# Two more row tiles of a spectral and feed-forward kernel normalised and multiplied in 64-row halves, one weight block loaded once, and the input loaded ahead of the constants

## The chip, the core and the metric

The kernel runs on one core of one Trainium2 chip. A core has TensorE (PE in the profile; its weight loads are PEld), VectorE (DVE), ScalarE (ACT), GpSimd (POOL) and SyncE (SP), which here only issues transfers. Each engine works through its instructions in a fixed order; semaphores make one wait for another. SBUF (128 partitions) holds the data, PSUM (8 banks of 128 x 512 float32) takes what TensorE computes, and DMA engines move data. The metric is the device time of one execution in microseconds; lower is better.

## The reference

Two equal layers are applied to x of shape 1 x 2048 x 448 in bfloat16. Each adds a filter in the frequency domain and then a feed-forward block (FFN), both after a layer normalisation without gain:

```python
def _A_ref(x, w_r, w_i):
    X = jnp.fft.rfft2(x.astype(jnp.float32), axes=(-2, -1))
    X = X * (w_r + 1j * w_i)
    return jnp.fft.irfft2(X, s=(S, D), axes=(-2, -1)).astype(jnp.bfloat16)

def _B_ref(x, w1, b1, w2, b2):
    h = jnp.einsum("bsd,df->bsf", x, w1) + b1
    h = relu(h) ** 2
    return jnp.einsum("bsf,fd->bsd", h, w2) + b2

for layer in range(2):
    x = x + _A_ref(_layernorm(x), w_r, w_i)
    x = x + _B_ref(_layernorm(x), w1, b1, w2, b2)
```

S is 2048, D is 448, and the hidden width F is 1792 = 14 x 128.

## The kernel before

The 2048 rows are 16 row tiles of 128 rows. The transforms are matmuls with constant matrices (FA, TD, G, H, TI, FI and others) that are loaded at the start. The program goes through these stages:

- Start (0 to 17.7 us). The rows of x come into `xin` by four transfers on SP's queue and four on ACT's. Per tile: statistics (DVE, L825, or ACT, L847), a reversed copy XR (POOL, L707, into `VT`), a scaled constant `Fs` (POOL L718 or ACT L717), and five matmuls with it (stage A1).
- Spectral 1 (to 42.6 us): matmuls with TD, G and H, and between them products with the filter on DVE.
- Ramp 1 (to 50.2 us). Inverse stages TI and AI return x per pair of tiles: TI's matmuls, an eviction of 128 x 896 to `tmp` (ACT, L706), AI's matmuls, and a sum into `x_sb` (DVE, L1146). Then `ln_B` normalises.
- FFN 1 (to about 142 us). Rows go in four chunks of four tiles. `h_part` or `h_pairs` make the hidden rows of a chunk (14 blocks `fb` of 128 features), ACT applies ReLU, DVE squares, and `o_tile` multiplies a row tile by W2 in 14 matmuls of 448 columns.
- Spectral 2, ramp 2 (142 to 172.9 us) and FFN 2 (to 262.7 us), the same once more; rows leave at the end.

The first FFN matmul needs its rows transposed, in `yT`: four blocks of 128 columns per tile, the fourth with only 64 columns of data. Three ways lead there:

- Tiles 0 and 1: raw rows are flipped on TensorE by matmuls with J (`flip`) and evicted to `yT`. They are not normalised. The standard deviation and its rounding rest stand in two extra columns of x (L1163 on), so that b1 is added by two more rows of W1, and the output tile is multiplied by the squared reciprocal deviation (`r2`).
- Tiles 2 and 3: raw in the same way, but transposed by one DMA from `x_sb` on SP's queue.
- Tiles 4 to 15: `ln_rows` takes the root, the reciprocal, scales each tile into the buffer `xn` (it lies in `arena`, room for one pair), copies the 64 tail columns once more behind the row, and sends one DMA transpose per pair. The fourth block of `yT` then has its 64 rows in both partition halves.

`h_part` uses raw rows with 128-row blocks: four matmuls per block `fb`, each with two tiles (256 columns) as the moving operand. `h_pairs` uses normalised rows and splits the contraction of 448 into seven blocks of 64 rows, so that two matmuls, one on the lower and one on the upper half of the array, stand side by side; all four tiles (512 columns) move through, and b1 is added as a bias by the ReLU. For the fourth block the upper half needs rows 384 to 447 of W1 on partitions 64 to 127 (`W1u`). Before, these lie in `VT`, which the spectral stage uses, so that they are loaded again in each layer, by two transfers on SP's queue behind the transpose of tiles 6 and 7.

The order of each engine's instructions is not found by rule: a table `ORDER` holds, per engine, the numbers of the program's units, and the scheduler replays it. It picks the PSUM banks, adds the semaphore waits, and inserts dummy matmuls on `ones` (L1415) where it expects TensorE to idle. The table also sets the order of transfers on SP's queue and which engine evicts where two are allowed.

## Time and profile before

| What | Value |
|---|---|
| Runs | 266.54 us median of 3 (266.14 to 266.84) |
| Profiled execution | 266.92 us |
| Its span | 265.0 us |
| PE busy | 256.8 us (97%) |
| DVE busy | 204.5 us (77%) |
| ACT busy | 172.7 us (65%) |
| First matmul of FFN 1, of FFN 2 | 50.17 us, 172.87 us |
| Granted TensorE clock | 1.00 in every stretch |

The span is what the profiler recorded between the first and the last instruction; the execution's time has 1.9 us around it. PE's busy time includes pipelined matmuls, so the distance between two starts, and not the duration in a row, is what a matmul costs in a stream. In a timeline row the first number is the start, the second the time to the end of the group, and brackets give the idle time before it and what ended it.

### The profile page before, as it was taken

The numbers are of one execution on the slowest core, as the hardware profiler recorded it, in microseconds if no ns is written. First come the engines' busy times: TensorE is split into PE (matmuls) and PEld (weight loads), VectorE is DVE, ScalarE is ACT, GpSimd is POOL, SyncE is SP. The second block draws the span as 40 slices with busy tenths as digits, with TensorE's granted clock in tenths as the row PEclk, the third lists the DMA queues.
The fourth block names the chain that finished last, engine by engine and source line by source line (L and its number), as shares of the span: only waits on it lengthen the run. The fifth ranks groups of instructions, "written<-read, shape, count | busy, mean of one in ns | idle before, by whom it ended". The sixth has DMA issues, their size and how long they took to land.

```text
span 265.0 us, 5666 instructions
## 1 busy us (share of the span) xinstructions
PE 256.8 (97%) x2125; PEld 162.6 (61%) x2125; DVE 204.5 (77%) x658; ACT 172.7 (65%) x375; POOL 14.2 (5%) x32
## 2 busy tenths in 40 slices
PE   6999989999999999999999999999999999999996
PEld 2676768797544555665558756789654465554454
DVE  2978998999969983489998899899964069921662
ACT  5978897999449447893216889999634886121820
POOL 8840000000000000000000000000000000000000
PEclk9999999999999999999999999999999999999999
DMA  7999900032300214000000000022232000220053
GB/s 223 303 299 385 270 8 2 0 72 41 74 2 1 44 37 80 2 0 2 0 1 2 2 0 2 0 45 41 42 69 45 2 0 2 40 41 2 0 173 106
DMA packets 25531, 16.33 MB, mean 62 GB/s; under 512 B 18174, under 2 KB 24542, under 8 KB 25504
## 3 DMA queue, kind: packets, MB, share of 16 engines
q1 hardware_dynamic: 24768, 14.25, 19.9%
q10 hardware_dynamic: 576, 0.92, 1.0%
q0 software_dynamic: 160, 0.81, 0.9%
q8 instruction: 17, 0.28, 0.4%
q14 instruction: 10, 0.08, 0.1%
HBM read 10.46 MB, written 1.84 MB: 46 GB/s over the span
## 4 chain that ended last, share of the span: by engine, by line
PE 81%; DVE 8%; ACT 5%; DMA 2%; issue 2%; SPq 0%; POOL 0%; DVEq 0%; POOLq 0%
PE ps L681 81%; DVE tmp L735 6%; DMA xin<-in_A_x_dram 2%; DVE arena L735 2%; ACT VT L706 2%; ACT tmp L706 2%; ACT arena L706 1%; SPq L673 0%; ACT yT L706 0%; ACT mv L700 0%; DVE st L825 0%; PE ps L1415 0%; ACT Fs L717 0%; POOL Fs L718 0%; DVE VT L707 0%
## 5 line engine op out<-in xcount | busy, mean ns | idle before, releaser
L681 PE MATMUL ps<-yT,W_sb 64*128 64x512 bf16 (+1 forms) x770 | 90.3, 346 | 0.1
L681 PE MATMUL ps<-W_sb,arena 128*128 128x448 bf16 (+3 forms) x476 | 87.0, 342 | 0.0
L681 PEld LDWEIGHTS ps<-yT,W_sb 64*128 64x128 bf16 (+1 forms) x770 | 54.5, 95 | 31.9 <-ACT arena L700 1.3
L700 ACT ACTIVATE arena<-ps,b1col 128x512 bf16<-128x512 f32 x84 | 51.9, 689 | 28.8 <-PE ps L681 28.8
L681 PEld LDWEIGHTS ps<-W_sb,arena 128*128 128x128 bf16 x476 | 45.4, 98 | 38.5 <-DVE arena L735 1.5
L735 DVE TENSOR_TENSOR arena<-arena 128x512 bf16<-128x512 bf16 (+1 forms) x140 | 45.8, 366 | 24.7 <-ACT arena L700 24.5
L706 ACT ACTIVATE arena<-ps 128x448 bf16<-128x448 f32 (+1 forms) x41 | 26.0, 705 | 4.5 <-PE ps L681 4.4
L1170 ACT ACTIVATE VT<-x_sb 128x448 bf16<-128x448 bf16 x28 | 16.1, 580 | 16.4 <-DVE x_sb L1146 16.4
L700 ACT ACTIVATE mv<-mv,epst 128x1 f32<-128x1 f32 (+1 forms) x45 | 12.6, 296 | 17.0 <-DVE mv L826 14.0
L700 ACT ACTIVATE arena<-ps 128x256 bf16<-128x256 f32 x56 | 18.0, 386 | 0.6 <-PE ps L681 0.5
L706 ACT ACTIVATE XA<-ps 128x512 bf16<-128x512 f32 x26 | 14.5, 590 | 5.2 <-PE ps L681 5.1
L681 PE MATMUL ps<-arena,G_sb 128*128 128x448 bf16 (+1 forms) x84 | 16.9, 335 | 0.9 <-ACT arena L706 0.9
L1292 DVE SCALAR_TENSOR_TENSOR x_sb<-ps,mv,arena 128x448 bf16<-128x448 f32 (+2 forms) x13 | 8.3, 644 | 11.9 <-PE ps L681 11.8
L681 PE MATMUL ps<-H_sb,arena 128*128 128x256 bf16 x128 | 15.8, 273 | 1.2 <-DVE arena L735 0.6
L706 ACT ACTIVATE VT<-ps 128x1024 bf16<-128x1024 f32 (+2 forms) x20 | 14.0, 773 | 3.0 <-PE ps L681 3.0
L735 DVE TENSOR_TENSOR tmp<-arena,Wt 128x896 bf16<-128x896 bf16 x26 | 15.4, 623 | 0.6 <-ACT arena L706 0.4
L681 PE MATMUL ps<-yT,VT 64*128 64x512 bf16 x42 | 15.8, 376 | 0.0
L681 PEld LDWEIGHTS ps<-H_sb,arena 128*128 128x128 bf16 x128 | 11.7, 98 | 5.0 <-DVE arena L735 3.4
L681 PE MATMUL ps<-TD_sb,XA 112*128 112x112 bf16 (+3 forms) x232 | 14.3, 229 | 0.1
L681 PEld LDWEIGHTS ps<-TD_sb,XA 112*128 112x128 bf16 (+3 forms) x232 | 12.3, 103 | 2.8 <-ACT XA L706 0.5
L706 ACT ACTIVATE tmp<-ps 128x896 bf16<-128x896 f32 (+1 forms) x16 | 12.7, 853 | 1.1 <-PE ps L681 1.0
L681 PEld LDWEIGHTS ps<-arena,G_sb 128*128 128x128 bf16 x84 | 7.7, 98 | 6.5 <-ACT arena L706 1.5
(84 smaller groups left out, 299.6 us busy)
## 6 DMA issues: line engine op xcount, KB each, us to landing
out_dram<-x_sb SPq DMA_DIRECT2D x15, 112.0 KB, 1.8
W_sb<-in_B_w_dram SPq DMA_DIRECT2D x1, 1568.0 KB
W_sb<-in_B_w_dram SPq DMA_DIRECT2D x1, 1344.0 KB, 11.0
xin<-in_A_x_dram ACTq DMA_DIRECT2D x4, 224.0 KB, 6.4
xin<-in_A_x_dram SPq DMA_DIRECT2D x4, 224.0 KB, 8.7
H_sb<-c_H SPq DMA_DIRECT2D x1, 896.0 KB, 8.6
G_sb<-c_G SPq DMA_DIRECT2D x1, 672.0 KB, 6.9
...
```

The source lines that it names most:

```text
L681: return sch.add("pe", lambda e: e.matmul(_res(o), lhsT, rhs, start=start, stop=stop, skip_group_check=skip), [lhsT, rhs], [o], cost=cost, ...
L700: sch.add("act", lambda e: e.activation(o, _res(i), func, **kw), rd, [o], cost=c)
L706: op = sch.add(engs[0], lambda e: e.activation(o, _res(i), ACT.Copy) if h[0].eng == "act" else e.tensor_copy(o, _res(i)), [i], [o], cost=c ...
L735: sch.add(eng, lambda e: e.tensor_tensor(o, _res(a), b, op), [a, b], [o], cost=_free(o) / rate + 69.0)
L1170: op = sch.add("act", lambda e, i=i, o=o, x=x, h=h: e.activation(o, x, ACT.Square, accum_out=sd[:, i, 1:2]) if h[0].eng == "act" else e.sc ...
L1292: small(lambda e: e.scalar_tensor_tensor(out=o, in0=_res(i), scalar=rs[0] if rs else 1.0, in1=xi, op0=ALU.add if t >= 4 and last else ALU. ...
```

## The change

A constant `RAW = 2` takes the place of the fixed 4 that divides raw from normalised tiles. Tiles 2 and 3 go through `ln_rows`, and in chunk 0 their hidden rows through `h_pairs` with 256 columns; tiles 0 and 1 stay with `h_part`. `W1u` has a buffer of its own and is loaded once at the start. The table `ORDER` is new for every engine.

```diff
+RAW = 2
 ORDER = {
...
-        W1u = VT[:].rearrange("p a b t c j -> p (a b) (t c j)")
...
+        W1u = sb("W1u", [P, FB // 2, P])
...
-        memset(x_sb[:, 0:4, D:4 * P].bitcast(FP32), 0.0, eng="pool")
+        memset(x_sb[:, 0:RAW, D:4 * P].bitcast(FP32), 0.0, eng="pool")
...
+        dma("sp", W1u[64:128], B_w1[384:448, :].rearrange("r (i k c) -> r i k c", k=2, c=P)[:, :, 1, :])
...
-            if t >= 4:
+            if t >= RAW:
                 ln_rows(t, n, last)
...
-            if t < 4 and last:
+            if t < RAW and last:
...
-        def h_pairs(c):
-
-            tk = slice(4 * c, 4 * c + 4)
+        def h_pairs(c, t0, t1):
+
+            tk, w = slice(4 * c + t0, 4 * c + t1), (t1 - t0) * P
...
-                w = W1u[h, fb // 4, fb % 4 * P:(fb % 4 + 1) * P] if up and j == 3 else W1_sb[h, j, f]
-                op = mm(q[fb][lambda b: ps[:, b, :]], w, yT[h, tk, j, :], start, stop, unit=u)
+                k = W1u[h, fb // 2, :] if up and j == 3 else W1_sb[h, j, f]
+                op = mm(q[fb][lambda b: ps[:, b, 0:w]], k, yT[h, tk, j, :], start, stop, unit=u)
...
-                    hb = hbuf[c % 2][:, fb, :]
-                    act(hb, q[fb][lambda b: ps[:, b, :]], ACT.Relu, bias=b1col[:, fb:fb + 1])
+                    hb = hbuf[c % 2][:, fb, t0 * P:t1 * P]
+                    act(hb, q[fb][lambda b: ps[:, b, 0:w]], ACT.Relu, bias=b1col[:, fb:fb + 1])
...
-            rs = [r2[:, t, 0:1]] if t < 4 else [mv2[:, t, 3:4]] if last else []
+            rs = [r2[:, t, 0:1]] if t < RAW else [mv2[:, t, 3:4]] if last else []
...
-                if t == 6:
-                    for k, w in ((0, 3), (3, 1)):
-                        dma("sp", W1u[64:128, k:k + w, 0:min(4 * P, FF - 4 * P * k)],
-                            B_w1[384:448, 4 * P * k:min(FF, 4 * P * (k + w))].rearrange("r (k c) -> r k c", k=w),
-                            after=[yT[:, 6, 0, :]])
             for c in range(4):
                 if c > 0:
-                    h_pairs(c)
-                for t0, t1 in ((0, 2), (2, 4)) if c == 0 else ():
+                    h_pairs(c, 0, 4)
+                for t0, t1 in ((0, RAW), (RAW, 4)) if c == 0 else ():
-                    h_part(c, range(4 if t0 == 0 else 1), t0, t1)
-                    for fb in range(4 if t0 == 0 else 1, FB):
+                    if t0 > 0:
+                        h_pairs(c, t0, t1)
+                        continue
+                    h_part(c, range(4), t0, t1)
+                    for fb in range(4, FB):
                         h_part(c, (fb,), t0, t1)
```

Where the orders differ is shown at four places. The first is the start of SP's queue, before the change:

```order
L673 DMA xin<-in_A_x_dram 128x896
L673 DMA FA_sb<-c_FA 128x256
L673 DMA xin<-in_A_x_dram 128x896 x2
L673 DMA Wt<-in_A_w_r_dram 128x2x225
L673 DMA TI_sb<-c_TI 112x896
L673 DMA xin<-in_A_x_dram 128x896
```

And after it:

```order
L672 DMA xin<-in_A_x_dram 128x896 x2
L672 DMA FA_sb<-c_FA 128x256
L672 DMA xin<-in_A_x_dram 128x896 x2
L672 DMA TD_sb<-c_TD 128x896
L672 DMA GN_sb<-c_GN 128x512
```

The second x transfer now stands ahead of FA, and the fourth ahead of Wt and TI.

The second place is ACT's queue in ramp 1, from its first evictions of TI (`tmp`) through the flipped rows (`yT`) and the squares (L1170) to the ReLU of the first hidden rows (L700, 128x256), before:

```order
L706 ACTIVATE tmp<-ps 128x896 x6
L700 ACTIVATE mv<-mv,epst 128x1 x2
L706 ACTIVATE yT<-ps 128x384 x2
L706 ACTIVATE yT<-ps 128x128 x2
L706 ACTIVATE tmp<-ps 128x896
L1170 ACTIVATE VT,mv<-x_sb 128x4x112 x2
L700 ACTIVATE arena<-ps 128x256
```

And after:

```order
L705 ACTIVATE tmp<-ps 128x896 x4
L1170 ACTIVATE VT,mv<-x_sb 128x4x112
L705 ACTIVATE tmp<-ps 128x896
L1170 ACTIVATE VT,mv<-x_sb 128x4x112
L699 ACTIVATE mv<-mv,epst 128x1 x2
L705 ACTIVATE yT<-ps 128x384
L705 ACTIVATE tmp<-ps 128x896
L705 ACTIVATE yT<-ps 128x128
L705 ACTIVATE tmp<-ps 128x896
L1170 ACTIVATE VT,mv<-x_sb 128x4x112
L705 ACTIVATE yT<-ps 128x128
```

The seventh eviction of TI and three squares, two of them of tiles 0 and 1 (which DVE computed before), stand ahead of the last flipped block; one flipped block of 384 columns is evicted by DVE.

The third place is the same queue in ramp 2, before:

```order
L706 ACTIVATE tmp<-ps 128x224 x2
L706 ACTIVATE tmp<-ps 128x896 x3
L700 ACTIVATE mv<-mv,epst 128x1 x2
L706 ACTIVATE tmp<-ps 128x896 x3
L1170 ACTIVATE VT,mv<-x_sb 128x4x112 x2
```

And after:

```order
L705 ACTIVATE tmp<-ps 128x896 x5
L699 ACTIVATE mv<-mv,epst 128x1
L705 ACTIVATE yT<-ps 128x384
L699 ACTIVATE mv<-mv,epst 128x1
L705 ACTIVATE tmp<-ps 128x896 x2
L705 ACTIVATE yT<-ps 128x128
L1170 ACTIVATE VT,mv<-x_sb 128x4x112 x2
```

Two flipped blocks that DVE evicted before are on ACT, the two small evictions of 224 columns are not, and a seventh eviction of 896 has come in.

The fourth place is TensorE at the start of FFN 2, from the first hidden rows (`yT,W_sb` 128x256) to the first output tile (`W_sb,arena`), before:

```order
L681 MATMUL ps<-yT,W_sb 128x256 x32
L681 MATMUL ps<-TI_sb,VT 128x112 x8
L681 MATMUL ps<-yT,W_sb 128x256 x8
L681 MATMUL ps<-tmp,FI_sb 128x2x112 x4
L681 MATMUL ps<-yT,W_sb 128x256 x12
L681 MATMUL ps<-tmp,FI_sb 128x2x112 x4
L681 MATMUL ps<-yT,W_sb 128x256 x28
L681 MATMUL ps<-tmp,FI_sb 128x2x112 x4
```

And after, down to the first of the fourteen halves on `W1u`:

```order
L680 MATMUL ps<-yT,W_sb 128x256 x24
L680 MATMUL ps<-tmp,FI_sb 128x2x112 x4
L680 MATMUL ps<-yT,W_sb 128x256 x20
L680 MATMUL ps<-tmp,FI_sb 128x2x112 x4
L680 MATMUL ps<-yT,W_sb 128x256 x4
L680 MATMUL ps<-tmp,FI_sb 128x2x112 x4
L680 MATMUL ps<-yT,W_sb 128x256 x15
L680 MATMUL ps<-yT,W1u 128x256
L680 MATMUL ps<-yT,W_sb 128x256 x7
L680 MATMUL ps<-yT,W1u 128x256
```

TI of the last pair has left this stretch for the ramp, 48 of the 56 matmuls of tiles 0 and 1 stand among three AI groups, and from the ninth of the next fifteen on they are halves of tiles 2 and 3.

15 lines of the change are left out of this document (7 added, 8 removed), and 89 rows, old and new, of the table ORDER.

## The prediction

> **What bounds the kernel now.** I read the page first (busy shares and the chain that ended last), then the table of stretches, then the timeline around the places that the change touches.
>
> ```profile
> PE 256.8 (97%) x2125; PEld 162.6 (61%) x2125; DVE 204.5 (77%) x658; ACT 172.7 (65%) x375; POOL 14.2 (5%) x32
> ...
> PE 81%; DVE 8%; ACT 5%; DMA 2%; issue 2%; SPq 0%; POOL 0%; DVEq 0%; POOLq 0%
> ...
> 8.90:14.00 5.10, 4.70 (x42) 3.98 (x43) 5.10 (x27) 5.10 (x17) 4.19 (x10) 1.00 0.99 270
> 27.20:43.00 15.80, 14.58 (x112) 10.21 (x111) 15.38 (x30) 13.54 (x19) 0.00 (x0) 1.00 0.36 101
> 43.00:50.20 7.20, 6.92 (x88) 5.81 (x89) 6.67 (x22) 6.57 (x13) 0.00 (x0) 1.00 0.01 2
> 50.20:60.00 9.80, 9.80 (x92) 8.84 (x93) 9.31 (x25) 9.21 (x29) 0.00 (x0) 1.00 0.23 49
> 60.00:70.00 10.00, 10.00 (x70) 6.61 (x69) 9.97 (x47) 8.56 (x31) 0.00 (x0) 1.00 0.28 53
> 172.40:190.00 17.60, 17.59 (x161) 14.74 (x162) 17.55 (x63) 17.11 (x53) 0.00 (x0) 1.00 0.17 34
> ```
>
> The first two lines make TensorE the bound: 256.8 us busy in a span of 265.0, and 81% of the chain that ended last. The stretches (busy time of PE, its weight loads, DVE, ACT and POOL, then granted clock, share and rate of the DMA engines) say where this is not so. In the spectral stage (27.2 to 43.0) DVE is busy 15.38 of 15.80 us and PE 14.58. In the ramp that follows (43.0 to 50.2) PE, DVE and ACT are all above 90%, and in the first stretch of each FFN (50.2 to 60, 172.4 to 190) PE is full and DVE and ACT nearly so. So matmul time saved in an FFN shortens the end, but every step added there on ACT or DVE is at its own limit. The clock is 1.00 everywhere and enters no term.
>
> **The change, part by part.** *1. x ahead of the constants.*
>
> ```profile
> 13.17 0.27 PE L681 MATMUL ps<-Fs,m 128*128 128x256 bf16 x1
> 13.83 0.28 PE L681 MATMUL ps<-Fs,xin 128*128 128x256 bf16 x1 [0.39 <-POOL Fs L718]
> ...
> 12.76 0.56 POOL L707 COPY VT<-xin 128x448 bf16<-128x448 bf16 x1 [0.91 <-DMA xin<-in_A_x_dram]
> 13.29 3.21 POOL L718 TENSOR_SCALAR Fs<-FA_sb,rstd 128x256 bf16<-128x256 bf16 x7
> ...
> 15.20 0.16 DVE L856 RECIPROCAL rstd<-mv 128x2 f32<-128x2 f32 x1
> ```
>
> PE's matmuls here start 0.11 us apart, so the next one was due at 13.28 and came at 13.83: 0.55 us lost. POOL's Fs was late because its reversed copy had stood 0.91 us before an x tile. With x ahead of Wt and TI on SP's queue the wait goes, and first-stage transforms end 0.55 us earlier. What is late next is DVE's statistics: its last reciprocal stands at 15.20 and DVE is full from 8.9 to 14.0, so more than the copy's own 0.9 cannot come. Bounds 0 (the statistics hold the same place) and −0.9; I take −0.55. Constants loaded later (TI, H, half of Wt) are used from 27 us on, where the DMA engines are busy 36%; I cost them, and the W1u load that joins them at the start, at nothing: if that cover went, the wait would show in the spectral stage.
>
> *2. Spectral 1 and 2.* Nothing is added; both run at DVE's pace (15.38 of 15.80) and shift with what stands ahead. 0, by bounds ±0.3, which is the idle of that row (0.42) and some.
>
> *3. Tiles 2 and 3 in halves, layer 1.*
>
> ```profile
> 50.17 3.22 PE L681 MATMUL ps<-yT,W_sb 128*128 128x256 bf16 x28
> 53.23 0.55 PE L681 MATMUL ps<-tmp,FI_sb 128*128 128x224 bf16 x4
> 53.61 2.78 PE L681 MATMUL ps<-yT,W_sb 128*128 128x256 bf16 x24
> ...
> 78.08 1.67 PE L681 MATMUL ps<-yT,W_sb 64*128 64x512 bf16 x13
> 79.59 1.67 PE L681 MATMUL ps<-yT,W_sb 64*128 64x512 bf16 x13
> 84.13 1.46 PE L681 MATMUL ps<-yT,W_sb 64*128 64x512 bf16 x12
> 85.52 0.56 PE L681 MATMUL ps<-tmp,FI_sb 128*128 128x224 bf16 x4
> 176.43 0.55 PE L681 MATMUL ps<-TI_sb,VT 112*128 112x112 bf16 x8
> 176.82 1.04 PE L681 MATMUL ps<-yT,W_sb 128*128 128x256 bf16 x8
> ...
> L681 PEld LDWEIGHTS ps<-yT,W_sb 64*128 64x128 bf16 x546 | 32.9, 94 | 29.2 <-ACT arena L700 1.3 <-issue 0.9
> L681 PEld LDWEIGHTS ps<-TI_sb,VT 112*128 112x128 bf16 x128 | 8.2, 97 | 1.6 <-DVE VT L707 1.0 <-ACT VT L706 0.3 <-ACT tmp L706 0.2
> ```
>
> A full 256-wide matmul takes (53.23 − 50.17)/28 = 0.109 us. Fourteen half matmuls of 512 columns (13 in the row and the one from VT) take 79.59 − 78.08 = 1.51 us, 0.108 each, since two halves share the array; half the columns give 0.054. Now 56 × 0.109 = 6.10 us, then 98 × 0.054 = 5.29: saved 0.8 us, and I take 0.76 with 0.0545 each. The 256-wide half is in no row. From below it cannot beat 0.054; from above it is bounded by weight loads: full loads of 97 ns stand behind each 112-wide matmul of TI, of which eight take 176.82 − 176.43 = 0.39 us, 0.049 each, so loads overlap to that pace and 0.056 is a fair upper end, −0.6. The Trainium skill has a rule against this, in "TensorE: Matmul & The Clock Gate", section "LDWEIGHTS (loading the stationary operand)": a load costs its 128 columns over 1.2, 107 ns, however few rows it has. One load after another would make 98 × 0.107 = 10.5 us, 4.4 more than now in each layer; by this trace (94 ns for the 64-row load, so the length agrees) loads do overlap, and I stay with 0.76.
>
> A change of row mode costs 85.52 − 84.13 − 12 × 0.108 = 0.09 us. In layer 1 chunk 1's halves now follow directly, so none is added.
>
> Against that stands ACT, which must deliver both flipped tiles before the first FFN matmuls.
>
> ```profile
> 43.66 4.97 ACT L706 ACTIVATE tmp<-ps 128x896 bf16<-128x896 f32 x6 [0.51 <-PE ps L681]
> 48.46 0.52 ACT L700 ACTIVATE mv<-mv,epst 128x1 f32<-128x1 f32 x2
> 48.83 1.58 ACT L706 ACTIVATE yT<-ps 128x384 bf16<-128x384 f32 x4
> 51.10 0.58 ACT L1170 ACTIVATE VT<-x_sb 128x448 bf16<-128x448 bf16 x1
> 51.66 0.57 ACT L1170 ACTIVATE VT<-x_sb 128x448 bf16<-128x448 bf16 x1
> ```
>
> Before, the queue is 6 evictions of 896 (0.80 each), 2 roots (0.37), 4 evictions of yT (1.48 from start to end); PE began at 50.17. Now 7 evictions, 3 squares (0.56 apart), 2 roots and three yT evictions (some 1.0 us) stand ahead of the last flipped block: 43.66 + 5.6 + 1.7 + 0.4 + 1.0 = 52.3. That block is needed by the thirteenth matmul, 12 × 0.109 = 1.3 us in, so PE in effect starts at 51.0, +0.85; waits of the aux columns on DVE can make it +1.3, no wait at all 0. I take +1.1. Inverse stage AI for tile 6 is done in that ramp instead of later: 53.61 − 53.23 = −0.38. The o tiles now follow the first half at once and may wait on DVE's squares, DVE being full: +0.1 (0 to 0.2). Sum for layer 1: 1.1 − 0.38 − 0.76 + 0.1 = +0.05 (−1.15 to +0.4).
>
> *4. The same, layer 2.*
>
> ```profile
> 171.44 2.53 ACT L706 ACTIVATE tmp<-ps 128x896 bf16<-128x896 f32 x3
> ...
> 172.87 3.69 PE L681 MATMUL ps<-yT,W_sb 128*128 128x256 bf16 x32
> ```
>
> ACT ends its six large evictions at 173.8 (2.4 after 171.44). Now one more (0.8), a flipped 384 (0.5) and a flipped 128 (0.25) precede the point that PE waits for, and two small ones of 224 are gone (0.74 at most): 174.65 to 175.4, less the 1.3 of the first twelve matmuls, against 172.87: +0.5 to +1.2, taken +0.85. TI of tile 14 moves into the ramp, −0.39; halves −0.76; two more mode changes, since AI and o tiles follow, +0.2. Sum −0.1 (−1.0 to +0.4), if yT of tiles 2 and 3 is there.
>
> *5. Normalising tiles 2 and 3.*
>
> ```profile
> DMA to landing us min/median/max: 3.0/3.1/3.1
> ...
> L717 ACT ACTIVATE arena<-x_sb,rstd 128x448 bf16<-128x448 bf16 x9 | 5.9, 663 | 0.8 <-DVE rstd L1215 0.6
> L718 DVE TENSOR_SCALAR arena<-x_sb,rstd 128x448 bf16<-128x448 bf16 x15 | 4.7, 333 | 2.7 <-DMA yT<-arena 2.7
> L700 ACT ACTIVATE arena<-ps 128x256 bf16<-128x256 f32 x56 | 18.0, 386 | 0.6 <-PE ps L681 0.5
> L700 ACT ACTIVATE arena<-ps,b1col 128x512 bf16<-128x512 f32 x84 | 51.9, 689 | 28.8 <-PE ps L681 28.8
> L706 ACT ACTIVATE XA<-ps 128x512 bf16<-128x512 f32 x26 | 14.5, 590 | 5.2 <-PE ps L681 5.1
> ```
>
> Each layer gets two scalings (0.66 on ACT, 0.33 on DVE), and the transpose, 3.1 us from issue to landing, leaves behind them instead of before. In layer 2: last flip about 175.1, two squares and a root to 176.4, reciprocal, scaling and tail copy to about 177.7, landing at 180.8. PE reaches the halves after 56 × 0.109 and three AI groups of 0.38 from 173.7: 180.95. Just covered; 0, by bounds 0 and +0.5. In layer 1 four AI groups and two o tiles stand between: covered. ReLU in halves takes the bias as an operand: at most 0.689 − 0.590 = 0.10 us each, 1.4 us of ACT a layer, hidden behind eight PSUM banks and the slack of 60 to 70 (8.56 of 10); 0.
>
> *6. W1u loaded once.* Two small transfers per layer leave SP's queue behind the transpose of tiles 6 and 7. PE waits there for nothing but yT, so 0; the transposes behind them could start 0.6 us earlier, also hidden.
>
> Sum: −0.55 + 0 + 0.05 − 0.1 + 0 + 0 = −0.6. The profiled execution took 266.92 around its span of 265.0, so 264.4 and 266.3; against the median of the runs, 266.54, it is 265.9.
>
> **The rivals.** *A, faster by more:* ACT does not hold a ramp, because its moved squares fill time in which it waited for PE anyway (0.51 us in the first row of ramp 1; 6.57 of 7.20 busy speaks against). One ramp without its slip gives −0.6 − 1.0 and 264.9, both 263.9.
>
> *B, slower:* in layer 2 yT of tiles 2 and 3 comes late. Its reciprocal, scaling and tail copy stand in DVE's order, and DVE is 17.55 of 17.60 us busy there; four steps of 0.6 us ahead of them that I place behind put the landing 2.5 us later, 2.3 past the need: 268.2. It decides against the change from 1.6 us of lateness (0.15 of cover, 0.6 of gain and 0.8 for the threshold). Against it: the order puts them right behind the first squares.
>
> *C, slower:* the halves at 256 columns are held by their loads. Each 94 ns one after another makes 98 × 0.094 = 9.2 us, +3.1 for −0.76, 3.9 a layer: 273.7. The 107 ns of the Trainium skill ("TensorE: Matmul & The Clock Gate", section "LDWEIGHTS (loading the stationary operand)") would make it some 276. Against it are the TI groups, whose full loads pass at 0.049.
>
> *D, no effect at the start:* DVE's statistics hold the first stage; then −0.05 is left: 266.5.
>
> **How the numbers follow.** A measurement of this kernel tells about 0.3% (0.8 us) from no change. The forecast has 0.41 (0.11 of it beyond −0.8, 0.28 within, 0.02 above); A 0.32, all faster; B 0.13, of which 0.11 slower and 0.02 within; C 0.03, slower; D 0.11, of which 0.09 within and 0.02 slower. So faster 0.43, same 0.39, slower 0.18. The range goes from 264.4, between one and both ramps of A, to 267.6, which takes D with its +0.4 bounds and the smaller half of B; larger B, C and both ramps of A together are left out with under 0.2. Signs being mixed, the forecast's own range is 265.1 to 266.7.
>
> **What would show it.** Part 1: no POOL wait for x near 12.8, and PE's first stage ending near 17.1. Part 3: FFN matmuls starting near 51.3 against 50.17, less 0.55, and 98 halves in 5.3 us. Part 4: start at some 0.8 us later relative to the ramp's first TI, and PE entering the halves without a wait. Wrong would be: a gap of PE before those halves (B), a spacing of about 94 ns in them (C), FFN starts that do not slip (A).

## The result, and the profile after

The changed kernel takes 267.65 us (median of 8 runs, 267.39 to 268.0) against 266.39 us before (median of 8, 265.94 to 267.01). The ratio is 1.0046, with a 95% interval from 1.0034 to 1.0059: it is slower by 0.46%, where 265.9 us and a gain were forecast. The profiled execution took 268.0 us around a span of 266.0 us, 1.0 us more than the span before, so the profile shows most of the loss.

The busy shares and the chain that ended last, of the kernel after:

```profile
PE 256.7 (97%) x2215; PEld 165.8 (62%) x2215; DVE 202.5 (76%) x654; ACT 175.3 (66%) x378; POOL 14.1 (5%) x32
...
PE 79%; DVE 15%; issue 2%; DMA 2%; ACT 1%; DVEq 0%
```

TensorE is as busy as before (256.8 us), and DVE's share of the chain has grown from 8% to 15%. Where the time went is seen only by stage. The next two views are the table of stretches for the kernel before and the kernel after, each cut at the same six places: from the first matmul of TD to the first of TI (spectral 1), to the first FFN matmul (ramp 1), to the first matmul of TD in layer 2 (FFN 1), the same two stages again, and FFN 2 up to DVE's last instructions. The columns are start and end, length, then busy time and count of PE, its weight loads, DVE, ACT and POOL, the granted clock, and the DMA engines' share and rate.

```profile
17.75:42.65 24.90, 23.69 (x199) 17.02 (x199) 22.26 (x44) 20.63 (x33) 0.00 (x0) 1.00 0.62 205
42.65:50.17 7.52, 7.24 (x88) 5.95 (x89) 6.92 (x23) 6.89 (x14) 0.00 (x0) 1.00 0.01 2
50.17:142.24 92.07, 92.06 (x717) 57.06 (x718) 78.65 (x307) 56.85 (x139) 0.00 (x0) 1.00 0.13 26
142.24:166.78 24.54, 23.07 (x276) 16.39 (x275) 22.47 (x53) 21.25 (x34) 0.00 (x0) 1.00 0.01 2
166.78:172.87 6.09, 6.03 (x76) 5.03 (x77) 5.08 (x18) 5.50 (x11) 0.00 (x0) 1.00 0.00 0
172.87:262.01 89.14, 89.14 (x670) 51.16 (x667) 55.65 (x162) 47.93 (x112) 0.00 (x0) 1.00 0.17 41
```

And of the kernel after:

```profile
17.27:42.62 25.35, 23.61 (x199) 17.18 (x199) 22.43 (x45) 20.34 (x32) 0.00 (x0) 1.00 0.63 188
42.62:51.20 8.58, 7.87 (x97) 6.49 (x97) 8.11 (x25) 7.91 (x17) 0.00 (x0) 1.00 0.01 2
51.20:142.48 91.28, 91.23 (x759) 56.30 (x756) 76.80 (x302) 56.69 (x138) 0.00 (x0) 1.00 0.14 24
142.48:167.31 24.83, 22.72 (x276) 16.73 (x275) 22.30 (x55) 21.51 (x35) 0.00 (x0) 1.00 0.01 1
167.31:174.21 6.90, 6.69 (x85) 5.54 (x85) 6.28 (x21) 6.36 (x12) 0.00 (x0) 1.00 0.01 2
174.21:262.80 88.59, 88.36 (x702) 53.24 (x702) 53.64 (x158) 48.88 (x112) 0.00 (x0) 1.00 0.18 40
```

Read against each other, row by row, and against the terms of the prediction:

| Stage | Forecast (us) | Measured (us) |
|---|---|---|
| Start, to the first TD matmul | -0.55 | -0.48 |
| Spectral 1 | 0 | +0.45 |
| Ramp 1 | +1.1 | +1.06 |
| FFN 1 | -0.38 - 0.76 + 0.1 = -1.04 | -0.79 |
| Spectral 2 | 0 | +0.29 |
| Ramp 2 | +0.85 | +0.81 |
| FFN 2, to DVE's last instructions | -0.39 - 0.76 + 0.2 = -0.95 | -0.55 |
| From there to the end of the span | 0 | +0.21 |
| Sum | -0.6 (rounded) | +1.0 |

The start, both ramps and the sign of both FFNs came as forecast. What was missed is 0.74 us in the two spectral stages, for which the sum had 0, about 0.65 us of gain that did not arrive in the FFNs, and 0.21 us at the end.

Three places of the kernel after carry this. First TensorE, in its timeline: the ramp's end, the halves of layer 2, and what follows them.

```profile
49.62 0.55 PE L680 MATMUL ps<-TI_sb,VT 112*128 112x112 bf16 x8 [0.55 <-DVE x_sb L738]
50.12 0.59 PE L1413 MATMUL ps<-ones 128*128 128x512 bf16 x2
51.20 5.52 PE L680 MATMUL ps<-yT,W_sb 128*128 128x256 bf16 x48
...
182.37 0.27 PE L680 MATMUL ps<-yT,W1u 64*128 64x256 bf16 x1
186.20 0.27 PE L680 MATMUL ps<-yT,W1u 64*128 64x256 bf16 x1
187.06 0.56 PE L680 MATMUL ps<-tmp,FI_sb 128*128 128x224 bf16 x4
187.84 0.54 PE L680 MATMUL ps<-tmp,FI_sb 128*128 128x224 bf16 x4 [0.23 <-ACT arena L699]
```

In ramp 1 PE stands 0.55 us ahead of TI's matmuls, and runs dummy matmuls on `ones` before the first FFN matmul. The profile names a copy at L738 for the 0.55 us, but TI's matmuls read nothing of that column. Just ahead of it DVE ends two sums into `x_sb`, which empty PSUM, 0.06 us before the copy ends:

```profile
48.20 1.27 DVE L1146 SCALAR_TENSOR_TENSOR x_sb<-ps,mv,xin 128x448 bf16<-128x448 f32 x2
49.39 0.14 DVE L738 CAST x_sb<-mv 128x1 bf16<-128x1 f32 x1
```

So DVE holds PE there, and the likelier reading is that TI waits for a bank that these sums empty. In layer 2 the halves come from 182.37 to 186.20 in five groups of fourteen: 3.83 / 70 = 0.0547 us each. The AI group after them should take 0.38 us and the next one stand at 187.44. It stands at 187.84, so 0.40 us are lost to a PSUM bank that ACT had not yet emptied (the bracket in the last row shows 0.23 of it, since the row before it counts PE as busy until 187.06 + 0.56 = 187.62).

Second, ACT in that stretch. Then layer 1: PE's weight loads at the place where they wait, and ACT's ReLUs just ahead:

```profile
183.16 5.63 ACT L699 ACTIVATE arena<-ps,b1col 128x256 bf16<-128x256 f32 x14
```

```profile
72.23 0.33 PEld L680 LDWEIGHTS ps<-yT,W_sb 64*128 64x128 bf16 x6 [0.44 <-ACT arena L699]
70.92 1.63 ACT L699 ACTIVATE arena<-ps,b1col 128x512 bf16<-128x512 f32 x3 [0.61 <-PE ps L680]
```

Fourteen ReLUs with bias take 5.63 us. Divided by fourteen that is 0.402 us, but the 5.63 us also hold the tail of the last one and two places where ACT waits for PE (0.10 us before the second, 0.03 us before the tenth). Where they stand back to back they start 0.357 us apart: five steps take 1.78 us, from 184.53 to 186.32. PE makes what one of them reads in 7 x 0.0547 = 0.383 us, so here ACT is the faster of the two. In layer 1 the loads wait 0.44 us for ACT (0.32 us of PE's matmuls), and ACT itself had stood 0.61 us for PE right before. In both layers, then, PE waits for an engine that has just waited for PE.

### The profile page after: what moved, and what is told of

Its sections match the earlier page's. It is cut to its first block, busy times and chain, and to the rows that moved or that the text cites. A ratio compares the mean times of both kernels' runs of the same rounds, so it can differ in the third digit from the quotient of the medians.

```text
span 266.0 us, 5883 instructions
## 1 busy us (share of the span) xinstructions
PE 256.7 (97%) x2215; PEld 165.8 (62%) x2215; DVE 202.5 (76%) x654; ACT 175.3 (66%) x378; POOL 14.1 (5%) x32
## 4 chain that ended last, share of the span: by engine, by line
PE 79%; DVE 15%; issue 2%; DMA 2%; ACT 1%; DVEq 0%
PE ps L680 78%; DVE tmp L734 8%; DVE arena L734 2%; DMA xin<-in_A_x_dram 2%; PE ps L1413 1%; DVE x_sb L1146 1%; ACT arena L699 1%; DVE st L825 1%; ACT arena L705 1%; DVE VT L734 0%; DVE arena L706 0%; DVE VT L1171 0%; DVE yT L706 0%; DVE VT L706 0%; DVE x_sb L1292 0%
## 5 line engine op out<-in xcount | busy, mean ns | idle before, releaser
L680 PE MATMUL ps<-yT,W_sb 64*128 64x512 bf16 (+2 forms) x840 | 88.9, 339 | 0.1
L699 ACT ACTIVATE arena<-ps,b1col 128x512 bf16<-128x512 f32 (+1 forms) x112 | 63.4, 638 | 32.3 <-PE ps L680 32.1
L680 PEld LDWEIGHTS ps<-yT,W_sb 64*128 64x128 bf16 (+1 forms) x840 | 56.2, 94 | 28.2 <-ACT arena L699 1.7
L1292 DVE SCALAR_TENSOR_TENSOR x_sb<-ps,mv,arena 128x448 bf16<-128x448 f32 (+2 forms) x15 | 9.6, 648 | 16.1 <-PE ps L680 16.0
L705 ACT ACTIVATE XA<-ps 128x512 bf16<-128x512 f32 (+1 forms) x28 | 14.8, 578 | 9.2 <-PE ps L680 9.0
L1170 ACT ACTIVATE VT<-x_sb 128x448 bf16<-128x448 bf16 x30 | 17.7, 594 | 4.6 <-DVE x_sb L1146 4.6
L680 PE MATMUL ps<-yT,W1u 64*128 64x512 bf16 (+1 forms) x56 | 19.6, 349 | 0.0
L705 ACT ACTIVATE tmp<-ps 128x896 bf16<-128x896 f32 x14 | 12.2, 928 | 1.2 <-PE ps L680 1.2
L716 ACT ACTIVATE arena<-x_sb,rstd 128x448 bf16<-128x448 bf16 x9 | 6.1, 674 | 8.9 <-DVE arena L1205 3.5
L1413 PE MATMUL ps<-ones 128*128 128x512 bf16 (+2 forms) x30 | 10.2, 459 | 1.7 <-POOL ones L747 1.0
```

Of the source, the lines that this page charges most:

```text
L680: return sch.add("pe", lambda e: e.matmul(_res(o), lhsT, rhs, start=start, stop=stop, skip_group_check=skip), [lhsT, rhs], [o], cost=cost, ...
L699: sch.add("act", lambda e: e.activation(o, _res(i), func, **kw), rd, [o], cost=c)
L705: op = sch.add(engs[0], lambda e: e.activation(o, _res(i), ACT.Copy) if h[0].eng == "act" else e.tensor_copy(o, _res(i)), [i], [o], cost=c ...
L716: op = sch.add(engs[0], lambda e: e.activation(o, i, ACT.Copy, scale=s) if h[0].eng == "act" else e.tensor_scalar(o, i, s, 1.0, op0=ALU.mu ...
L1170: op = sch.add("act", lambda e, i=i, o=o, x=x, h=h: e.activation(o, x, ACT.Square, accum_out=sd[:, i, 1:2]) if h[0].eng == "act" else e.sc ...
L1292: small(lambda e: e.scalar_tensor_tensor(out=o, in0=_res(i), scalar=rs[0] if rs else 1.0, in1=xi, op0=ALU.add if t >= RAW and last else AL ...
```

## The experiments

Kernels that ran together are compared with the kernel before on the same chip. Where only the order of instructions was edited, the diff shows rows of the order. "After" is the changed kernel, "before" the old one.

### The start: x first, alone

SP's transfers in before's program take after's order; every other queue is as before.

```diff
 L673 DMA xin<-in_A_x_dram 128x896
+L673 DMA xin<-in_A_x_dram 128x896
 L673 DMA FA_sb<-c_FA 128x256
 L673 DMA xin<-in_A_x_dram 128x896 x2
+L673 DMA TD_sb<-c_TD 128x896
+L673 DMA GN_sb<-c_GN 128x512
...
 L673 DMA Wt<-in_A_w_r_dram 128x2x225
-L673 DMA TI_sb<-c_TI 112x896
-L673 DMA xin<-in_A_x_dram 128x896
```

> The kernel before, with x ahead of the constants on SP's queue as in the changed kernel and nothing else. In the changed kernel the first stage ended 0.48 us earlier (first TD matmul at 17.27 against 17.75), yet the ramp began at 42.62 against 42.65. Theory 'order': the new order of the spectral stage on PE, DVE and ACT swallowed it; then here the first TD matmul stands near 17.3, the ramp near 42.2, and the time is 0.45 us below the kernel before, about 265.9. Rival 'fixed': something that the order does not set (a constant's arrival, DVE's pace from a fixed point) holds the spectral stage; then the ramp stays at 42.65 and the time at 266.4.

Measured: 266.29 us against 266.49, ratio 0.9988 (0.9973 to 1.0003). In its profile the first TD matmul stands at 16.89 us, 0.86 ahead of before. TensorE and DVE at that place, in the timelines of this kernel:

```profile
16.89 2.60 PE L681 MATMUL ps<-TD_sb,XA 128*64 128x224 bf16 x40
20.91 0.69 DVE L735 TENSOR_TENSOR tmp<-arena 128x448 bf16<-128x448 bf16 x2 [0.30 <-ACT arena L706]
179.72 2.79 PE L681 MATMUL ps<-yT,W_sb 128*128 128x256 bf16 x24 [0.22 <-DMA yT<-x_sb]
```

Spectral 1 kept its length (24.89 us from the first TD to the first TI matmul), so what the start gains is not lost behind it. Layer 2's stretch from the first FFN matmul to chunk 1 grew from 25.29 to 25.68 us, because the transpose of tiles 2 and 3 came late (third row). The start varies between executions: over all profiles of this study the first TD matmul stands at 17.09 to 18.05 us under before's order on SP (5 profiles, mean 17.54) and at 16.64 to 17.34 under after's (10 profiles, mean 16.96). That is 0.58 us earlier on average; the medians of this run alone show 0.2, which cannot be told from nothing.

### W1u loaded once, alone, and with two edits more

Before's program with a buffer for `W1u`, and nothing else:

```diff
-        W1u = VT[:].rearrange("p a b t c j -> p (a b) (t c j)")
+        W1u = sb("W1u", [P, FB // 2, P])
...
+        dma("sp", W1u[64:128], B_w1[384:448, :].rearrange("r (i k c) -> r i k c", k=2, c=P)[:, :, 1, :])
```

> The kernel before with W1's upper copy loaded once into a buffer of its own, and nothing else: two loads per layer leave SP's queue. Theory 'hidden': within 0.3 us of the kernel before (266.5), every stage interval within 0.05 us. Rival 'the load at the start delays a constant, or the later transposes gain': a start or spectral stage longer by 0.3 us or more, or a chunk shorter by as much.

Measured: 266.52 us against 266.29, ratio 1.0003 (0.9989 to 1.0016). Every stage has its old length (24.90, 7.52, and 25.29 from the first FFN matmul of layer 2 to chunk 1). Only the end differs: from the start of DVE's last two instructions to the end of the span it takes about 3.2 us, against 3.0 before. Of these 0.2 us, 0.18 lie behind the landing of SP's last output transfer: the span ends 0.49 us after it in the three kernels that load `W1u` in each layer, and 0.67 us after it in all twelve that load it once. SP ends by passing a row of waits, 0.06 us apart. In before the last output's wait is the last of the row (264.52 us, span 265.0); in after it stands three places earlier, and three more follow it (265.35, then 265.41, 265.47, 265.53, span 266.0). Loading `W1u` once takes three transfers off SP's queue, 57 in place of 60.

The second kernel adds x first, and in layer 2 puts an AI group ahead of the hidden rows of tiles 2 and 3:

```diff
 L680 MATMUL ps<-tmp,FI_sb 128x2x112 x4
-L680 MATMUL ps<-yT,W_sb 128x256 x28
-L680 MATMUL ps<-tmp,FI_sb 128x2x112 x4
-L680 MATMUL ps<-yT,W_sb 128x256 x28
+L680 MATMUL ps<-yT,W_sb 128x256 x4
+L680 MATMUL ps<-tmp,FI_sb 128x2x112 x4
+L680 MATMUL ps<-yT,W_sb 128x256 x52
 L680 MATMUL ps<-tmp,FI_sb 128x2x112 x4
```

> The kernel before with three things: x ahead of the constants, W1's upper copy loaded once, and in layer 2 AI of tiles 8 and 9 placed ahead of the hidden rows of tiles 2 and 3, so that PE has 0.38 us more to do while their transpose lands (it took 4.6 and 5.0 us instead of 3.1 in two profiles, and PE waited 0.6). Theory 'start and cover add up': first TD matmul near 17.0, no wait of PE on yT in layer 2, and the time 0.3 to 0.8 us below the kernel before: 265.7 to 266.2. Rival 'the start's gain is noise of its DMAs and AI comes too early for DVE': 266.4 or more.

Measured: 266.42 us against 266.29, ratio 1.0005 (0.9994 to 1.0016). Layer 2's stretch to chunk 1 takes 25.62 us, 0.33 more than before, so the group moved ahead did not win back what the late transpose costs. `W1u` costs nothing in the stages, as forecast; the 0.2 us at the end come with it.

### Ramp 1: squares back on DVE

After, with the squares of tiles 0 and 1 on DVE and the flipped blocks ahead of the last two evictions on ACT, as before's order had them. ACT's rows:

```diff
-L705 ACTIVATE tmp<-ps 128x896 x4
-L1170 ACTIVATE VT,mv<-x_sb 128x4x112
-L705 ACTIVATE tmp<-ps 128x896
-L1170 ACTIVATE VT,mv<-x_sb 128x4x112
+L705 ACTIVATE tmp<-ps 128x896 x5
 L699 ACTIVATE mv<-mv,epst 128x1 x2
-L705 ACTIVATE yT<-ps 128x384
-L705 ACTIVATE tmp<-ps 128x896
-L705 ACTIVATE yT<-ps 128x128
-L705 ACTIVATE tmp<-ps 128x896
+L705 ACTIVATE yT<-ps 128x384 x2
+L705 ACTIVATE yT<-ps 128x128 x2
+L705 ACTIVATE tmp<-ps 128x896 x2
```

> The changed kernel, with only ramp 1 put back: DVE squares tiles 0 and 1 again, ACT evicts both flipped 384 blocks, and all yT evictions stand ahead of the evictions of TI for tiles 8 and 12 and of tile 2's squares. Theory 'ACT's queue holds the ramp': the first FFN matmul moves from 51.20 to about 50.3 and the time falls by about 0.9 us, to 266.75. Rival 'DVE or the AI chain holds the ramp': with two squares (1.1 us) more on DVE the first FFN matmul stays within 0.3 us of 51.2 and the time stays at 267.6.

Measured: 270.12 us against 266.49, ratio 1.0135 (1.0114 to 1.0156). The ramp did not shrink; it grew from 8.58 to 10.23 us. Its stretch, and PE's wait in it, in the profile of this kernel:

```profile
42.70:52.93 10.23, 9.10 (x100) 6.67 (x101) 9.62 (x29) 7.31 (x15) 0.00 (x0) 1.00 0.01 2
```

```profile
50.58 0.55 PE L680 MATMUL ps<-TI_sb,VT 112*128 112x112 bf16 x8 [0.65 <-DVE x_sb L738]
```

ACT is busy 7.31 of 10.23 us, DVE 9.62. With the squares on DVE, PE waits longer at the same place behind DVE's sums (0.65 us instead of 0.55), and FFN 1 grows too, from 91.28 to 92.10 us. That ACT's queue alone holds this ramp is refuted.

### Ramps and FFNs: less work on ACT, less work on DVE

After, with the squares taken over 112 of 448 columns:

```diff
-                o = VT[:, :, :, i].rearrange("p a b c j -> p (a b) (c j)")[:, :, 0:D // 4]
-                x = x_sb[:, i, 0:D].rearrange("p (a c) -> p a c", a=4)
+                o = VT[:, :, :, i].rearrange("p a b c j -> p (a b) (c j)")[:, 0, 0:D // 4]
+                x = x_sb[:, i, 0:D // 4]
```

> The changed kernel, order untouched, with the same short squares (some 0.25 us less of ACT each, 30 of them on ACT in all). Theory 'ACT sets the ramps and the first chunk': FFN 1 starts near 50.3 after a ramp at 42.6 and the time falls by 1.5 us, to 266.1. Rival 'DVE sets them': less than 0.5 us, 267.2 to 267.6.

Measured: 267.47 us against 266.65, ratio 1.0024 (1.0012 to 1.0037). Ramp 1 stays at 8.58 us and ramp 2 at 6.90. Layer 1's stretch from the first FFN matmul to chunk 2 falls from 46.39 to 46.28 only, layer 2's to chunk 1 from 25.08 to 25.07, and PE's wait of 0.39 us ahead of the AI group of layer 2 is still there.

After, with the butterflies of the inverse stage done for one tile of each pair:

```diff
-                    tt(w[:, :, :, i], y[:, :, :, 1], y[:, :, :, 0], ALU.subtract if i else ALU.add)
+                    tt(w[:, 0:1, :, i], y[:, 0:1, :, 1], y[:, 0:1, :, 0], ALU.subtract if i else ALU.add)
...
-                    tt(y[:, :, i], w[:, :, 0], w[:, :, 1], ALU.add if i else ALU.subtract)
+                    tt(y[:, 0:1, i], w[:, 0:1, 0], w[:, 0:1, 1], ALU.add if i else ALU.subtract)
```

> The changed kernel, order untouched, with the butterflies of AI (four DVE operations of 0.385 us per pair, six pairs a layer) done for one tile of each pair only (the other tile's x is wrong): about 4 us less of DVE per layer. Theory 'DVE sets the ramps and the first chunk': the time falls by 2 us or more, to 265.6 or below. Rival 'ACT sets them': less than 0.7 us, above 266.9. If this and the shorter squares each give half, both engines are at their limit together.

Measured: 268.5 us against 266.65, ratio 1.007 (1.0048 to 1.0093). Ramp 1 falls by 0.16 us only, to 8.42; its long wait is still there:

```profile
49.10 0.55 PE L680 MATMUL ps<-TI_sb,VT 112*128 112x112 bf16 x8 [0.51 <-DVE x_sb L738]
```

Layer 2's stretch to chunk 1 falls from 25.08 to 24.71 us, but layer 1's to chunk 2 grows from 46.39 to 47.30. Neither engine's load by itself sets the ramp: squares over a quarter of the columns do nothing, butterflies of half the tiles give 0.16 us. What remains is the chain that passes from one to the other (TI on PE, eviction on ACT, butterfly on DVE, AI on PE, sum on DVE, square on ACT, root on ACT, columns on DVE, flip on PE), or two queues that are both full: with less on DVE, DVE is still busy 7.63 of 8.42 us and ACT runs without a break from 43.31 us on. Both readings fit the runs. No run cut the chain or relieved both engines at once, so the reason is argued and not shown.

In layer 2 this kernel shows something else. The fourteen ReLUs come at after's pace, but PE's two AI groups follow each other without a wait, and the 0.37 us by which the stretch is shorter are that wait:

```profile
183.42 5.65 ACT L699 ACTIVATE arena<-ps,b1col 128x256 bf16<-128x256 f32 x14
187.32 0.97 PE L680 MATMUL ps<-tmp,FI_sb 128*128 128x224 bf16 x8
```

So the wait for ACT's ReLU is not one for ACT's pace. In layer 1 the stretch grows in two waits of AI groups behind DVE (0.56 us lost at 56.57, 0.26 at 58.46); why they come there was not found.

### The halves under the old order, and with less on ACT

After's program, with before's order on every engine as far as the two have the same units. TensorE's rows around the start of FFN 1:

```diff
-L680 MATMUL ps<-yT,W_sb 128x256 x48
-L680 MATMUL ps<-tmp,FI_sb 128x2x112 x4
-L680 MATMUL ps<-yT,W_sb 128x256 x8
+L680 MATMUL ps<-tmp,FI_sb 128x2x112 x4
+L680 MATMUL ps<-J_sb,x_sb 128x128 x2
+L680 MATMUL ps<-yT,W_sb 128x256 x28
+L680 MATMUL ps<-tmp,FI_sb 128x2x112 x4
```

> The changed program (tiles 2 and 3 normalised, halves, W1u once) under the order of the kernel before on every engine, with only the replaced steps put at the places of those they replace. Theory 'the new order is what costs, the halves themselves gain': FFN starts near 50.2 and 172.9 as before, 0.76 us saved per layer in the halves, less 0.4 of ReLU stalls and 0.3 of mode changes and late yT each: 266.3, and clearly below the changed kernel (267.65). Rival 'the halves or the normalised rows cost': at or above 267.6 although the FFNs start as early as before.

Measured: 270.51 us against 266.49, ratio 1.0145 (1.0121 to 1.0169). Spectral 1, ramp 1, spectral 2 and ramp 2 have before's lengths (24.90, 7.52, 24.54, 6.08 us), so all of the loss is in the FFNs, where 13.38 us to the first output tile became 15.18. TensorE's rows there:

```profile
58.99 0.50 PE L680 MATMUL ps<-yT,W_sb 64*128 64x256 bf16 x6 [0.15 <-ACT arena L699]
...
59.77 0.27 PE L680 MATMUL ps<-yT,W1u 64*128 64x256 bf16 x1
60.80 0.27 PE L680 MATMUL ps<-yT,W1u 64*128 64x256 bf16 x1
61.56 0.27 PE L680 MATMUL ps<-yT,W1u 64*128 64x256 bf16 x1
62.74 0.27 PE L680 MATMUL ps<-yT,W1u 64*128 64x256 bf16 x1
```

The fourteen halves from 60.80 to 61.56 take 0.76 us, the ones on either side 1.03 and 1.18. All 98 took from 58.56 to 65.65, 7.1 us instead of the 98 x 0.0547 = 5.4 that PE needs. The halves are faster on PE, but in this order two scalings and squares stand among the ReLUs that empty their banks, ACT is busy 5.98 of these 7.1 us, and PE waits. The ramps of this kernel are as short as before's under the new program, so it is the new order, and not the new program, that lengthens them.

The same with the squares over 112 of 448 columns, the edit of the run with less on ACT above:

> The changed program under the order of the kernel before (270.51), with every square sum taken over 112 of the 448 columns, so that ACT has some 0.25 us less for each of about 14 squares a layer (the normalisation is wrong by that). Theory 'ACT's queue is what PE waits for in the halves' (there PE's weight loads wait 4.7 us in all for ReLUs): the halves run faster and the time falls by 2 us or more, to 268.5 or below. Rival 'the order of PSUM banks or latency holds them': within 0.7 us of 270.5.

Measured: 269.43 us against 266.65, ratio 1.0103 (1.0074 to 1.0132): 2.78 us over before on its chip, against 4.02 with whole squares on another. FFN 1 to the first output tile falls from 15.18 to 14.87 us, FFN 2 from 16.37 to 15.76. ACT's load accounts for a part of the wait, here where the squares stand among the ReLUs.

### What a matmul less is worth in before

Before's program with 7 of 56 matmuls of tiles 2 and 3 left out per layer, 7 x 0.109 = 0.76 us of PE, as much as the halves save:

```diff
-                for blk in ((3,) if i else (0, 1, 2)):
+                for blk in ((3,) if i else (0, 1) if t0 == 2 and fb % 2 else (0, 1, 2)):
```

> The kernel before with 7 of the 56 full matmuls of tiles 2 and 3 left out in each layer (block 2 of every second feature block; those hidden rows are wrong), orders and all other work unchanged: 7 x 0.109 = 0.76 us less for TensorE per layer, the same as the halves save. Theory 'TensorE alone is the bound there': the time falls by 1.5 us, from 266.5 to 265.0. Rival 'ACT and DVE are as full as TensorE in that stretch (14.02 and 14.15 of 14.20 us in layer 2)': it falls by 0.5 us or less, 266.0 to 266.5.

Measured: 265.96 us against 266.65, ratio 0.9975 (0.9958 to 0.9991): 0.7 us of the 1.5 us offered. Layer 1's stretch to chunk 2 falls by 0.44 us (47.55 to 47.11). In layer 2 the first FFN matmul to chunk 1 grows from 25.29 to 25.51, since here too the transpose is late:

```profile
179.91 2.36 PE L681 MATMUL ps<-yT,W_sb 128*128 128x256 bf16 x20 [0.64 <-DMA yT<-x_sb]
```

So even without a change of order, PE time taken out of these stretches does not all come back: 0.44 of 0.76 us in the layer without that wait. ACT is not what keeps the rest there. The first output tile comes 12.65 us after the first FFN matmul instead of 13.38, which is 0.73 of the 0.76 us; the 0.3 us are lost right behind, where the output tile's weight loads wait 0.54 us for a square on DVE that ends at 62.95.

### The ReLUs among the squares

After, with the scaling of tile 5 and squares put behind ReLUs, so that no ReLU waits behind them. ACT's rows in layer 2:

```diff
 L699 ACTIVATE arena<-ps 128x256
+L699 ACTIVATE arena<-ps,b1col 128x256 x7
+L716 ACTIVATE arena<-x_sb,rstd 128x448
 L1170 ACTIVATE VT,mv<-x_sb 128x4x112
-L716 ACTIVATE arena<-x_sb,rstd 128x448
-L699 ACTIVATE arena<-ps,b1col 128x256 x14
+L699 ACTIVATE arena<-ps,b1col 128x256 x7
```

> The changed kernel with four small ACT steps moved behind the ReLUs of the halves: in layer 2 the scaling of tile 5 and a square of tile 6 behind the eighth ReLU, in layer 1 the squares of tiles 11 and 13. Theory 'ReLUs with the halves make ACT the bound, and PE waits for PSUM banks' (gaps of 0.4 us at 72.2 and at 187.4): both gaps close and the time falls by 0.8 us, to 266.85; if only one closes, 0.4. Rival 'the gaps are filled later anyway': time unchanged at 267.65 (within 0.2).

Measured: 269.17 us against 266.49, ratio 1.0103 (1.0081 to 1.0125). Layer 1's stretch to chunk 2 is unchanged (46.39). Layer 2's to chunk 1 grows from 25.08 to 26.47 us, because a copy on DVE needs that scaling and everything on DVE stands behind it:

```profile
186.25 0.20 DVE L738 COPY arena<-arena 128x128 bf16<-128x128 bf16 x1 [2.04 <-ACT arena L716]
```

After again, with a smaller edit. In layer 1 the ReLUs of f blocks 10 and 11 go ahead of that of block 12, in layer 2 a square goes behind the ReLUs:

```diff
 L699 ACTIVATE arena<-ps,b1col 128x512 x2
-L699 ACTIVATE arena<-ps,b1col 128x256
-L1170 ACTIVATE VT,mv<-x_sb 128x4x112
-L699 ACTIVATE arena<-ps,b1col 128x256 x2
-L1170 ACTIVATE VT,mv<-x_sb 128x4x112
+L699 ACTIVATE arena<-ps,b1col 128x256 x3
+L1170 ACTIVATE VT,mv<-x_sb 128x4x112 x2
```

> The changed kernel, with only ACT's order touched at two places: in layer 1 the ReLUs of f blocks 10 and 11 stand ahead of that of block 12, as PE's order has them (0.33 us of PE in the profile of after stands behind a PSUM bank there, 0.44 each at 72.2), and in layer 2 the scaling 1028 is put behind the last ReLU-feeding group of tiles 2 and 3 (0.54 us of PE waits at 187.8). Theory (the feed-forward halves' missing gain went into these PSUM-bank waits): the wait of 0.44 at 72.2 goes, first FFN matmul to chunk 2 of layer 1 falls from 46.39 to about 45.95, layer 2's first FFN matmul to chunk 1 from 25.08 to about 24.7, and the kernel from 267.65 to about 266.85. Rival (ACT's rate of ReLUs, not their order, sets the pace of these stretches): the waits move to a later matmul, both intervals stay within 0.1, and the time stays at 267.4 to 267.7.

Measured: 268.06 us (267.55 to 268.44, 4 runs) against 266.07, ratio 1.0075 (1.0055 to 1.0095). The intervals are those of after to 0.01 us: 46.40 for 46.39, 25.09 for 25.08. Both waits stand where they were, in PE's loads of layer 1 and its matmuls of layer 2:

```profile
71.90 0.33 PEld L680 LDWEIGHTS ps<-yT,W_sb 64*128 64x128 bf16 x6 [0.44 <-ACT arena L699]
...
187.51 0.54 PE L680 MATMUL ps<-tmp,FI_sb 128*128 128x224 bf16 x4 [0.23 <-ACT arena L699]
```

The theory that the rows moved here make these waits fell. In layer 1 ACT's row ahead of it explains why:

```profile
70.58 1.27 ACT L699 ACTIVATE arena<-ps,b1col 128x512 bf16<-128x512 f32 x2 [0.61 <-PE ps L680]
```

ACT first stands 0.61 us for PE, then has ReLUs of 512 columns one after another. The second ends at 70.58 + 1.27 = 71.85 us, and PE's load starts at 71.90. Both stand ahead of the ReLUs that were moved, so moving those could not help. In layer 2 the square moved away (the expectation speaks of a scaling) lets ACT start earlier, and it then stands 0.29 us for PE inside the fourteen ReLUs:

```profile
183.47 4.99 ACT L699 ACTIVATE arena<-ps,b1col 128x256 bf16<-128x256 f32 x13 [0.29 <-PE ps L680]
```

PE's wait at 187.51 is as long as in after all the same, so ACT is not short of time there. What is left is which ReLU frees the bank that the AI group takes. In after that is the eleventh of the fourteen (187.23 to 187.70). By the recorded order the tenth empties hidden block 10, for which ACT waits until 186.84, and only the eleventh empties block 9, whose halves PE had finished at about 186.0, 0.8 us earlier. With the two the other way round the bank would have come free about 0.36 us earlier, an estimate from the spacing of the ReLUs. This is read from the order and the trace; no run has exchanged the two. That this kernel's runs lie above those of after, while all its intervals are equal, is not explained by the profile; the two ratios' intervals just overlap.

### Spectral stages under the old order

After with before's order in the start and both spectral stages, the second one merged where the two programs' units allow it. TensorE's rows in spectral 1:

```diff
-L680 MATMUL ps<-arena,G_sb 128x448 x11
+L680 MATMUL ps<-TD_sb,XA 128x224 x8
+L680 MATMUL ps<-arena,G_sb 128x448 x3
 L680 MATMUL ps<-arena,GN_sb 128x448
-L680 MATMUL ps<-TD_sb,XA 128x224 x4
-L680 MATMUL ps<-arena,G_sb 128x448 x4
-L680 MATMUL ps<-TD_sb,XA 128x224 x12
+L680 MATMUL ps<-arena,G_sb 128x448 x12
+L680 MATMUL ps<-TD_sb,XA 128x224 x8
```

> The changed kernel with the order of the kernel before in the start and in both spectral stages (PE, ACT, DVE, POOL); ramps, FFNs and SP's queue stay as changed. Under the new order the way from the first TD matmul to the first TI matmul took 25.35 and 24.83 us, under the old one 24.90 and 24.54, whatever the program. Theory 'the spectral order alone costs 0.75 us': 24.9 and 24.54 come back and the time falls to 266.9, still above the kernel before by some 0.4, which the ramps and first chunks keep. Rival 'the new spectral order is needed by what follows it (its ramp)': the ramps grow by as much, and the time stays at 267.6.

Measured: 267.28 us against 266.29, ratio 1.0029 (1.0017 to 1.0042). Spectral 1 is back at 24.90 us. The merged spectral 2 takes 25.19, more than either.

The last run puts before's order into the start and spectral 1 alone, on top of the kernel with the moved ReLUs:

> The kernel of the run a_gaps, and before's order on PE, DVE, ACT and POOL from the start to the end of the first spectral stage. Theory (the terms are separate and add): first TD to first TI matmul goes back from 25.35 to 24.90, the ramp and the feed-forward intervals are those of a_gaps, and the time is about 0.45 under that of a_gaps, 266.4, level with the kernel before. Rival (the first ramp gives the 0.45 back, since its fillers arrive in another order): the sum of the spectral stage and the ramp stays at 33.9 and the time that of a_gaps.

Measured: 266.9 us (8 runs, 266.87 to 267.07) against 266.07, ratio 1.0031 (1.002 to 1.0042). Spectral 1 takes 24.89 us, ramp 1 still 8.58, and all that follows is as in after: the term is separate, and it adds. The kernel stays slower than before. How the stage starts, in after and then in this kernel, from TensorE's and DVE's timelines:

```profile
17.27 1.76 PE L680 MATMUL ps<-TD_sb,XA 128*64 128x224 bf16 x32
19.33 0.94 PE L680 MATMUL ps<-TD_sb,XA 128*128 128x224 bf16 x8 [0.31 <-DVE arena L706]
21.80 0.84 DVE L734 TENSOR_TENSOR tmp<-arena 128x448 bf16<-128x448 bf16 x2
```

```profile
16.96 2.60 PE L680 MATMUL ps<-TD_sb,XA 128*64 128x224 bf16 x40
20.98 0.69 DVE L734 TENSOR_TENSOR tmp<-arena 128x448 bf16<-128x448 bf16 x2 [0.30 <-ACT arena L705]
```

With after's order PE makes 32 matmuls of TD and then waits for an eviction on DVE; DVE's first step of the filter, a sum or difference of two evicted halves ahead of the products, comes 21.80 - 17.27 = 4.53 us after the first TD matmul. With before's order 40 follow each other, and that step comes after 20.98 - 16.96 = 4.02 us. These 0.5 us by which DVE's stream starts later are about the 0.45 by which the stage is longer.

## Why the prediction was wrong

**Start, right.** -0.55 was forecast, -0.48 found in the profile, and -0.58 as the mean over all profiles. Rival D, that nothing happens at the start, fell.

**Spectral stages, the step that failed.** The term was "0, by bounds ±0.3", with the reason that both stages run at DVE's pace and only shift. They run at DVE's pace indeed, but when DVE's stream begins is set by PE's and the evictions' order ahead of it. The change has a new order there too, and it starts DVE half a microsecond later. The runs with before's order give 24.90 and 24.89 us back, which settles the 0.45 us of spectral 1; for the 0.29 us of spectral 2 the old order under the new program gives 24.54 again, in the run with the old order throughout. The order merged for that stage alone gave 25.19, so there the part of the order that costs the 0.29 us is not found. The diff of the program said nothing on this stage; the order did, and I had not costed its rows there.

**Ramps, right in size, the reason only in part.** +1.1 and +0.85 were forecast, +1.06 and +0.81 came. ACT's queue, from which the forecast was added up, ran as forecast: the last flipped block is evicted at 52.29 us, where 52.3 was said.

```profile
51.96 0.33 ACT L705 ACTIVATE yT<-ps 128x128 bf16<-128x128 f32 x1
```

But that ACT's queue alone holds the ramp is not so, and three runs say it: with the squares off ACT the ramp takes 1.65 us more, with shorter squares the same, with less on DVE 0.16 less. DVE is as full there as ACT (8.11 and 7.91 of 8.58 us), and the prediction had DVE in its upper bound only. That the size came out so well is in part luck. Rival A, no slip of the ramps, is refuted by both rows.

**Halves, right on PE, too high at the end.** 0.0545 us per half was taken, 0.0547 measured, so PE saves what was forecast. Rival C fell with it. The Trainium skill ("TensorE: Matmul & The Clock Gate", section "LDWEIGHTS (loading the stationary operand)") puts a load at its 128 columns over 1.2, 107 ns; the trace has loads of 94 ns, and halves at a spacing of 54.7 ns, so that the loads on the two halves of the array do not queue behind each other here. The section gives the price of one load and not a spacing, and for the sum the measured spacing decides.

What failed is the sentence that the ReLUs are "hidden behind eight PSUM banks", at 0. FFN 1 gave 0.79 of 1.04 us and FFN 2 0.55 of 0.95. In FFN 2 the missing 0.40 us is the wait of 0.40 us for a bank that a ReLU had not yet emptied. In FFN 1 PE waits 0.32 us for such a bank, and 0.25 us are missing. The price of a ReLU was not wrong: 0.10 us was put on each for the bias, and back to back they start 0.357 us apart with bias against 0.265 without (both in after, 256 columns). Nor is ACT slower than PE, which delivers what one ReLU reads in 0.383 us. ACT waits for PE among the same ReLUs. With a square less ahead of them it waits 0.29 us, and PE's wait stays. With less on DVE, PE's wait is gone at the same pace of ReLUs. It is the overlap that was wrong: at these two places PE comes to a bank whose ReLU has not ended, though ACT had itself waited for PE just before. In layer 2 the order has the ReLU of a block that PE finishes later stand ahead of the one that frees this bank. That this order makes the wait is the reading that fits, and no run has exchanged the two. In layer 1 the wait ends with a ReLU of 512 columns for which ACT had itself stood 0.61 us for PE, and its cause stays open.

The forecast's slack of 60 to 70 us, where ACT is busy 8.56 of 10 us, is one of layer 1. In layer 2 the prediction's own row for 172.40 to 190.00 in before has three engines full at once (17.59, 17.55 and 17.11 of 17.60 us), so that it had far less slack than the sentence took, though ACT's short waits for PE in after show that it did not run out. The Trainium skill says in "Perfetto Trace Analysis", section "Optimization Strategy", that in some kernels the most contended engine changes from one regime to the next. This trace shows one regime in which three engines are above 97%.

**Normalising, right.** In layer 2 PE enters the halves without a wait for `yT`, so rival B did not happen.

**W1u, right in the stages.** The term had 0 for the rest too, and 0.2 us came at the end of the span: 0.18 of them are the three waits of SP that follow the last output's.

The step that failed is thus an overlap and an order taken at 0: the spectral stages by +0.45 and +0.29 us, shown by the runs with before's order, and the ReLUs behind the banks by 0.32 and 0.40 us of waits, whose cause is argued in layer 2 and open in layer 1. Together the misses are +0.74 (spectral), +0.65 (FFNs) and +0.21 (end), 1.6 us, which is the distance from -0.6 to +1.0. The measured 267.65 us lies just above the range's upper end of 267.6; the chance of slower, 0.18, went almost wholly to rivals that did not happen.
